# A fourth block by half-size products: the second half batch of the first expert, with its sums of x made earlier

## The chip, the cores and the metric

The kernel runs on one core of a Trainium2 chip. Its time is the device time in microseconds (us) of one execution, as the median of several runs. The engines are TensorE (PE in the rows; PEld is its weight load), VectorE (DVE), ScalarE (ACT), GpSimd (POOL) and SyncE (SP), which issues the DMAs. Each works through its own queue in order; semaphores tie them together.

## The reference

Three layers follow one another: banded attention, a mixture of eight experts with gates normalised eight times by rows and columns, and a gated linear unit. The change lies in the first expert.

```python
logits = x @ w_gate                      # x: 1536 tokens x 512
P = np.exp(logits - logits.max())
for _ in range(8):
    P /= P.sum(1, keepdims=True) + 1e-09
    P /= P.sum(0, keepdims=True) + 1e-09
    P *= N / E
for e in range(E):                       # 8 experts
    h = np.maximum(x @ w1[e], 0.0)       # w1[e]: 512 x 1024
    ye = h @ w2[e]                       # w2[e]: 1024 x 512
    out += P[:, e:e + 1] * ye
```

## The kernel before

**Numbers in two parts.** Every float32 operand is split into a high part, rounded by ScalarE's copy, and a low part, which GpSimd gets by a subtraction (`split_one`, L222). A product takes three matmuls: high by high, high weights by low tokens, low weights by high tokens (`product`, L376; L382, L383, L384). The low part of the weights is so first read by the third matmul of a product. `wh`, `wl` are the parts of weights, `xh`, `xl` those of x, `hh`, `hl` those of the hidden layer.

**Visits.** An expert's 1024 hidden units are four blocks `f` of 256. A visit is one block over a set of tokens: the first layer (x by `w1`), relu, and the second layer (by `w2`), which adds into `acc`, 128 tokens at a time (a unit). A unit is 6 matmuls of 512 columns. The units of a visit are done during the next one. The list `visits` (L161) sets the order. For the first expert, before:

- visits 0 to 3: blocks 0 to 3 over the first 384 tokens of batch 0 (beside the attention);
- visits 4 to 7: blocks 3 to 0 over its other 384 tokens;
- visit 8: block 0 over all 768 tokens of batch 1, in two chunks, with the weights of visit 7 still in place;
- visits 9 to 11 (`H0` to `F0`): blocks 1, 2, 3 over batch 1, by half-size products.

From visit 12 on every visit of the other experts does both batches by half-size products.

**Two ways for the first layer.** The plain way (`run_visit`) takes 24 matmuls of 384 columns per chunk of 384 tokens, 48 for 768 tokens. The other (`pair`, L517) cuts weights and tokens into two by two blocks and does seven products instead of eight (`run(0)` to `run(6)`, 6 matmuls each, 42 in all). It needs seven left factors, made of the weights: four sums and differences of blocks (`sum_steps`, L280, on GpSimd, into `sg`), and seven splits (`form_step`, L291: ScalarE writes `wh`, GpSimd `wl`). And it needs right factors, made once per half batch of x (`trans_steps`, L1435): four whole blocks (L1452) and four differences (L1457) on VectorE, and four splits, three into `th`, `tl` and one back into a block of `xh`, `xl`. `trans_steps(1)` is for batch 1, `trans_steps(0)` for batch 0.

**What sets the order.** The order of each engine's queue is the order in which the code issues. Side work is cut into steps; a tick after each piece of TensorE's work issues some. `Paced` spreads its steps evenly over a number of ticks; `Planned` has a count for each tick. Up to visit 8 there are three such lists: `ahead` (the weights of the next visit), `side` (the gate's normalisation) and `other` (the sums of x). From visit 9 on `run_half` has its own list `ahead` and the ticks of `side`. `load` (L199) issues the two DMAs of 512 KB for the next weights on the SP queue, in order, each waiting until the old weights of that buffer have been read.

Of the kernel before, what the change touches and what calls it, by code (L numbers as in the profile page):

```python
# [81 lines left out]
def tile_global_local_attention__then__sinkhorn_moe__then__glu(  # L82
# [37 lines left out]
    CB = S // C  # L120
    FQ = 2 * P
    NQ = F // FQ
# [31 lines left out]
    def acc(t):  # L154
        return accs[t // TB][:, t % TB, :]
# [3 lines left out]
    chunks = [(t, 4) for t in range(0, NT, 4)]  # L159
    halves = [[(b * TB + t, TC) for t in range(0, TB, TC)] for b in range(B)]  # L160
    visits = []  # L161


    up, down = list(range(NQ)), list(reversed(range(NQ)))
    for order, over in (
        (up, halves[0][:1]), (down, halves[0][1:]), (down[3:], halves[1])
    ):
        for n, f in enumerate(order):
            again = len(visits) >= NQ and n < 2
            visits.append(  # L170
                dict(
                    kind="moe", e=0, f=f, chunks=over, slot=(len(visits) + len(visits) // NQ) % 2,
                    load=not again, start=n == 0,
                )
            )
    H0 = len(visits)
    for f in (down[2], *up[2:]):
        visits.append(
            dict(kind="fast", e=0, f=f, slot=len(visits) % 2, load=True, kept=f == down[2])
        )  # L180
    F0 = len(visits)
    for e in range(1, E):
        for f in range(NQ):
            visits.append(dict(kind="fast", e=e, f=f, slot=len(visits) % 2, load=True))
    for f in range(NFF):
        slot = 1 - visits[-1]["slot"]
        visits.append(dict(kind="gate", f=f, piece=3 * f))
        visits.append(dict(kind="val", f=f, piece=3 * f + 1, slot=slot))
    NA = NQ + 1
    NB0 = CB * NQ  # L190
# [8 lines left out]
    def load(b):  # L199
        at = state["load", b]  # L200
        state["load", b] += 1
        if at == len(queues[b]):
            for i in range(2):
                load_piece(2 * b + i)
            return
        for j, src in enumerate(queues[b][at]):
            nc.sync.dma_start(
                out=raw[b][:, j * 4 * FQ : (j + 1) * 4 * FQ].rearrange(
                    "p (k f) -> p k f", k=src.shape[0] // P
                ),  # L210
                in_=src.rearrange("(k p) f -> p k f", p=P),
            )
# [9 lines left out]
    def split_one(r, h, lo, eng=nc.gpsimd):  # L222
        nc.scalar.activation(out=h, in_=r, func=AF.Copy)  # L223
        eng.tensor_tensor(out=lo, in0=r, in1=h.bitcast(F32), op=ALU.subtract)  # L224
# [10 lines left out]
    def second_steps(n):  # L235

        vis = visits[n]
        if vis["kind"] == "gate" or vis.get("kept"):
            return
        if vis["kind"] == "val":  # L240
            r = piece(vis["piece"] + 1)
        else:
            r = raw[vis["raw"]][:, 4 * FQ : 8 * FQ]
        eng = nc.vector if n == G0 + 1 else nc.gpsimd
        yield from split_halves(r, wh[vis["slot"]][1], wl[vis["slot"]][1], eng)

    def first_steps(n):

        vis = visits[n]
        if vis["load"]:  # L250
            r = raw[vis["raw"]][:, 0 : 4 * FQ]
            yield from split_halves(r, wh[vis["slot"]][0], wl[vis["slot"]][0])

    def ahead_steps(n):


        if 1 < n < H0 - 1:
            yield from first_steps(n + 1)
        if visits[n]["load"]:
            yield from second_steps(n)  # L260
            yield lambda b=visits[n]["raw"]: load(b)
        if n == 1:
            yield from first_steps(n + 1)

    def form(i):
        a, col = (1, i) if i < 4 else (0, i - 4)
        cols = slice(col * FQ, (col + 1) * FQ)
        return wh[a][0][:, cols], wl[a][0][:, cols]

    def w1_blocks(n):  # L270
        r = first_raw(n).rearrange("p (k f c) -> p f k c", k=KD, f=2)
        return {(i, j): r[:, i, 2 * j : 2 * j + 2, :] for i in range(2) for j in range(2)}

    def tall(ap):
        return ap.rearrange("p (k c) -> p k c", k=2)

    def sums():
        return [tall(state["sums"][:, i * FQ : (i + 1) * FQ]) for i in range(4)]

    def sum_steps(n):  # L280

        a, (s1, s2, s3, s4) = w1_blocks(n), sums()
        for out, x, y, op in (
            (s1, a[1, 0], a[1, 1], ALU.add), (s2, s1, a[0, 0], ALU.subtract),
            (s4, a[0, 1], s2, ALU.subtract), (s3, a[0, 0], a[1, 0], ALU.subtract),
        ):
            yield lambda out=out, x=x, y=y, op=op: nc.gpsimd.tensor_tensor(
                out=out, in0=x, in1=y, op=op
            )

    def form_step(n, i):  # L291
        a, (s1, s2, s3, s4) = w1_blocks(n), sums()
        src = (a[0, 0], s1, s2, s4, s3, a[0, 1], a[1, 1])[i]
        h, lo = form(i)
        split_one(src, tall(h), tall(lo))
# [144 lines left out]
    def unit_second(n, t, at, j):  # L440
        vis = visits[n]
        ps = state["Y"].next()
        second(vis, hid[at], j, ps)
        a = acc(t)
        if vis["kind"] != "val":
            if n == H0 - 1:
                nc.scalar.activation(out=a, in_=ps, func=AF.Copy)
            elif vis.get("start"):
                nc.vector.tensor_copy(out=a, in_=ps)
            elif vis["e"] == 0:  # L450
                nc.vector.tensor_tensor(out=a, in0=ps, in1=a, op=ALU.add)
            else:
                gate = state["gate"]
                e = vis["e"]
                if e == 1 and vis["f"] == 0:
                    nc.vector.tensor_scalar(
                        out=a, in0=a, scalar1=gate[:, t, 0:1], scalar2=None, op0=ALU.mult
                    )
                nc.vector.scalar_tensor_tensor(  # L459
                    out=a, in0=ps, scalar=gate[:, t, e : e + 1], in1=a,  # L460
                    op0=ALU.mult, op1=ALU.add,
                )
        elif vis["f"] == 0:
            nc.vector.tensor_copy(out=a, in_=ps)
        elif vis["f"] < NFF - 1:
            nc.vector.tensor_tensor(out=a, in0=ps, in1=a, op=ALU.add)
        else:
            nc.vector.tensor_tensor(out=a, in0=ps, in1=a, op=ALU.add)
            nc.sync.dma_start(out=out[t * P : (t + 1) * P, :], in_=a)
# [11 lines left out]
    def flush(tick):  # L481
        pending, state["pending"] = state["pending"], []
        for unit in pending:
            unit_second(*unit)
            tick()
# [198 lines left out]
    def run_half(n, side):  # L684

        ahead = list(sum_steps(n + 1))
        if not visits[n]["kept"]:
            ahead += [*second_steps(n), lambda: load(visits[n]["raw"])]

        def slots(i):  # L690
            side()
            if ahead:
                ahead.pop(0)()
            if i:
                form_step(n + 1, i - 1)

        pair(n, 1, slots, {1: 1, 2: 1, 3: 1, 4: 1, 5: 2})
        for step in ahead:
            step()
        form_step(n + 1, 6)  # L700
# [75 lines left out]
    with tc.tile_pool(name="attn", bufs=1) as ap:  # L776
# [473 lines left out]
        with tc.If(banded > 0) as cmp:  # L1250
            with tc.tile_pool(name="banded", bufs=1) as fp:
# [30 lines left out]
                side = steps[begin + 1 :]  # L1282
                side = Planned(side, [0, *[1] * len(side)])
# [7 lines left out]
        with cmp.Else():  # L1291
            with tc.tile_pool(name="whole", bufs=1) as gp:
# [15 lines left out]
                for s in range(B * NP):  # L1308
# [17 lines left out]
                    for i in range(NB):  # L1326
# [29 lines left out]
                        for j in range(2):  # L1356
# [13 lines left out]
                            e = ga["e"]  # L1370
# [29 lines left out]
        kept = ["pending", "hid", ("load", 0), ("load", 1)]  # L1400
# [16 lines left out]
    fast = ctx.enter_context(tc.tile_pool(name="fast", bufs=1))  # L1417
    work = fast.tile([P, 8 * C], F32, name="work")
    kept = fast.tile([P, 6 * C], F32, name="kept")
# [144 lines left out]
                yield divided  # L1564

    first_, second_ = trans_steps(1), trans_steps(0)
    side = Paced(gate_steps(), 5 * (NB0 - NA) + 5 * CB + 13 * (F0 - H0) - 4)
    other = Planned([*first_[:-1], *second_], [2, 1] * 3 + [1] * 14)

    def both():  # L1570
        side.tick()
# [2 lines left out]
    for n in range(NA, H0):  # L1574
        if n < H0 - 1:
            run_visit(n, both, ahead_steps(n))
        else:
            ahead = [*sum_steps(H0), *(lambda i=i: form_step(H0, i) for i in range(4))]
            run_visit(n, both, ahead, pace=12)
    other.finish()  # L1580
    for i in range(4, 7):
        form_step(H0, i)
    first_[-1]()
    load(visits[H0]["raw"])

    state["after"], state["lows"] = [[] for _ in range(7)], []
    state.update(X=Ring(bank[0:2]), P2=bank[2], P5=bank[3], Y=Ring(bank[4:7]), G=Ring([bank[7]]))
    for n in range(H0, F0):
        run_half(n, side.tick)
    side.finish()  # L1590

    state["sums"] = work[:, 8 * FQ : 12 * FQ]
    state["Y"] = Ring(bank[4:8])
# [62 lines left out]
```

## Time and profile before

| | |
|---|---|
| three runs, median | 1387.54 us (1387.25 to 1387.89) |
| the profiled execution, its own time | 1388.02 us |
| its span, first to last instruction | 1386.2 us |
| TensorE busy | 1379.5 us |
| VectorE, GpSimd, ScalarE busy | 921.5, 667.9, 575.2 us |

The span is what the hardware profiler saw between the first and the last instruction; the execution's own time is 1.8 us more. Matmuls are pipelined: a row's duration overlaps the next row's, and what a matmul takes of TensorE's time is the step from its start to the next one's.

### The profile page before, as it was taken

How to read it: one execution, taken by the hardware profiler on the slowest of the kernel's cores; microseconds unless marked ns; L12 is line 12 of the kernel's file. 1: busy time of each engine (PE TensorE's matmuls, PEld its weight loads, DVE VectorE, ACT ScalarE, POOL GpSimd, SP SyncE). 2: the span in 40 equal slices, each digit the busy share in tenths (PEclk: the TensorE clock that was granted, in tenths of full speed). 3: DMA queues.
4: the chain of work that ended last, by engine and by line, in shares of the span. 5: the costliest groups of instructions: out<-in, count | busy, mean ns of one | idle time of the engine just before them, and what ended most of it. 6: DMA issues, size and time to landing. Idle time of an engine off the chain costs nothing.

```text
span 1386.2 us, 20767 instructions
## 1 busy us (share of the span) xinstructions
PE 1379.5 (100%) x7407; PEld 1233.9 (89%) x7407; DVE 921.5 (66%) x1770; ACT 575.2 (41%) x1372; POOL 667.9 (48%) x787
## 2 busy tenths in 40 slices
PE   9999999999999999999999999999999999999999
PEld 5888899999999999999999999999999899999998
DVE  7775866867666676767676676667665674555446
ACT  7785453333333333333333333333333464434441
POOL 5763685454445434454454444545453374443440
PEclk9999999999999999999999999999999999999999
DMA  7860112121213212121213212122120001010002
GB/s 172 206 163 13 61 62 77 53 77 54 76 54 107 73 57 76 54 77 54 77 54 107 77 54 76 55 75 71 59 91 31 16 32 46 16 47 31 31 1 92
DMA packets 99889, 93.73 MB, mean 68 GB/s; under 512 B 55104, under 2 KB 74304, under 8 KB 99776
## 3 DMA queue, kind: packets, MB, share of 16 engines
q1 hardware_dynamic: 98688, 91.98, 21.6%
q8 instruction: 60, 0.98, 0.3%
q14 instruction: 53, 0.43, 0.1%
q10 hardware_dynamic: 1088, 0.33, 0.1%
HBM read 79.71 MB, written 12.58 MB: 67 GB/s over the span
## 4 chain that ended last, share of the span: by engine, by line
PE 99%; DMA 1%; SPq 0%; issue 0%; ACTq 0%; DVE 0%; ACT 0%
PE bank L382 31%; PE bank L384 31%; PE bank L383 31%; PE bank L1078 2%; PE bank L1143 2%; PE bank L1128 1%; PE bank L934 1%; PE bank L713 0%; DMA kr<-in_k_dram 0%; DMA vo<-in_v_dram 0%; PE bank L1486 0%; PE bank L1490 0%; PE bank L835 0%; PE bank L1538 0%; SPq L794 0%
## 5 line engine op out<-in xcount | busy, mean ns | idle before, releaser
L459 DVE SCALAR_TENSOR_TENSOR acc<-bank,gate,acc 128x512 f32<-128x512 f32 x336 | 251.5, 749 | 228.5 <-PE bank L384 222.7
L224 POOL TENSOR_TENSOR wl<-raw,wh 128x256 fp32r<-128x256 f32 (+1 forms) x222 | 222.0, 1016 | 314.9 <-ACT wh L223 299.9
L382 PE MATMUL bank<-wh,hh 128*128 128x512 f32 x914 | 358.8, 393 | 0.0
L384 PE MATMUL bank<-wh,hl 128*128 128x512 f32 x914 | 357.6, 391 | 0.0
L383 PE MATMUL bank<-wl,hh 128*128 128x512 f32 x914 | 356.3, 390 | 0.0
L382 PE MATMUL bank<-xh,wh 128*128 128x384 f32 x744 | 252.0, 339 | 0.3 <-issue 0.3
L383 PE MATMUL bank<-xl,wh 128*128 128x384 f32 x744 | 249.9, 336 | 0.0
L384 PE MATMUL bank<-xh,wl 128*128 128x384 f32 x744 | 249.4, 335 | 0.0
L583 ACT ACTIVATE hh<-kept 128x384 fp32r<-128x384 f32 x177 | 92.9, 525 | 325.4 <-DVE kept L593 325.4
L384 PEld LDWEIGHTS bank<-wh,hl 128*128 128x128 f32 x914 | 171.5, 188 | 37.8
L224 POOL TENSOR_TENSOR wl<-work,wh 128x256 fp32r<-128x256 f32 x156 | 126.4, 814 | 149.4 <-ACT wh L223 149.3
L597 ACT ACTIVATE kept<-bank 128x384 f32<-128x384 f32 x249 | 122.0, 491 | 174.2 <-PE bank L384 172.8
L382 PEld LDWEIGHTS bank<-wh,hh 128*128 128x128 f32 x914 | 171.7, 188 | 22.5 <-issue 0.2
L383 PEld LDWEIGHTS bank<-wl,hh 128*128 128x128 f32 x914 | 171.8, 188 | 22.5
L382 PE MATMUL bank<-th,wh 128*128 128x384 f32 x498 | 167.7, 337 | 0.0
L384 PE MATMUL bank<-th,wl 128*128 128x384 f32 x498 | 167.3, 336 | 0.0
L383 PE MATMUL bank<-tl,wh 128*128 128x384 f32 x498 | 167.0, 335 | 0.0
L593 DVE TENSOR_TENSOR kept<-bank,kept 128x384 f32<-128x384 f32 x249 | 137.3, 552 | 38.4 <-PE bank L384 36.9
L382 PEld LDWEIGHTS bank<-xh,wh 128*128 128x128 f32 x744 | 139.7, 188 | 9.9 <-issue 0.9
L383 PEld LDWEIGHTS bank<-xl,wh 128*128 128x128 f32 x744 | 139.8, 188 | 9.3
L384 PEld LDWEIGHTS bank<-xh,wl 128*128 128x128 f32 x744 | 139.8, 188 | 0.0
L585 DVE SCALAR_TENSOR_TENSOR hl<-kept,hh 128x384 fp32r<-128x384 f32 x177 | 120.6, 682 | 1.9 <-ACT hh L583 1.8
(168 smaller groups left out, 1724.9 us busy)
## 6 DMA issues: line engine op xcount, KB each, us to landing
raw<-in_moe_w_dram SPq DMA_DIRECT2D x74, 512.0 KB, 4.3
glw<-work SPq DMA_DIRECT2D x36, 256.0 KB, 2.3
raw<-glw SPq DMA_DIRECT2D x18, 512.0 KB, 3.5
work<-in_moe_w_gate_dram SPq DMA_DIRECT2D x12, 512.0 KB, 3.8
work<-in_moe_w_val_dram SPq DMA_DIRECT2D x12, 512.0 KB, 4.0
work<-in_moe_w_out_dram SPq DMA_DIRECT2D x12, 512.0 KB, 3.8
qr<-in_q_dram SPq DMA_DIRECT2D x32, 96.0 KB, 2.8
vo<-in_v_dram SPq DMA_DIRECT2D x32, 96.0 KB, 2.7
```

Source lines behind the costliest of these rows:

```text
L224: eng.tensor_tensor(out=lo, in0=r, in1=h.bitcast(F32), op=ALU.subtract)
L382: nc.tensor.matmul(lhsT=ah, rhs=bh, start=first, stop=False, **mm)
L383: nc.tensor.matmul(lhsT=ah, rhs=bl, start=False, stop=False, **mm)
L384: nc.tensor.matmul(lhsT=al, rhs=bh, start=False, stop=end, **mm)
L459: nc.vector.scalar_tensor_tensor(out=a, in0=ps, scalar=gate[:, t, e : e + 1], in1=a, op0=ALU.mult, op1=ALU.add,)
L583: nc.scalar.activation(out=hh, in_=src, func=AF.Relu)
L585: lambda: nc.vector.scalar_tensor_tensor(out=hl, in0=src, scalar=0.0, in1=hh.bitcast(F32), op0=ALU.max, op1=ALU.subtract,)
L593: nc.vector.tensor_tensor(out=p, in0=ps, in1=kept, op=ALU.add)
L597: nc.scalar.activation(out=snap[:, i], in_=ps, func=AF.Copy)
L934: nc.tensor.transpose(ps[:, j * P : (j + 1) * P], raw_[u % QKB][:, j, :], ident)
L1078: nc.tensor.matmul(out=ps[j][:, lo:KW], lhsT=qT[rows, own], rhs=kT[rows, i % UB, lo:KW], start=True, stop=True,)
L1143: nc.tensor.matmul(out=ps[j * D : (j + 1) * D, at * P : (at + 1) * P], lhsT=vo[p][:, a, i - 1 + a, j, :], rhs=aT[:, j, a, :], start=(a == ...
```

## The change

Visit 8 is done by half-size products too. The list of visits loses its third group, and `H0` becomes 8; the half-size visits over batch 1 are now blocks 1, 0, 2, 3 (visits 8 to 11). `trans_steps(1)` is issued whole in visits 5 to 7, with the first six steps of `trans_steps(0)` behind it; the last six of that are issued in visits 8 to 11, at every eighth tick. The sums and the first four left factors of visit 8 are issued in visit 7, behind visit 7's own weights. Blocks 1 and 0 keep their `w2`, and their `w1` is loaded again. ScalarE's copy of a first result (L447) moves from visit 8's to the new visit 8's units. The slots of the weights swap.

```diff
     for order, over in (
-        (up, halves[0][:1]), (down, halves[0][1:]), (down[3:], halves[1])
+        (up, halves[0][:1]), (down, halves[0][1:])
     ):
...
-                    kind="moe", e=0, f=f, chunks=over, slot=(len(visits) + len(visits) // NQ) % 2,
+                    kind="moe", e=0, f=f, chunks=over, slot=len(visits) % 2 ^ (len(visits) >= NQ),
...
-    for f in (down[2], *up[2:]):
+    for f in (*down[2:], *up[2:]):
         visits.append(
-            dict(kind="fast", e=0, f=f, slot=len(visits) % 2, load=True, kept=f == down[2])
+            dict(
+                kind="fast", e=0, f=f, slot=1 - len(visits) % 2, load=True,
+                start=f == down[2], kept=f in down[2:],
+            )
         )
...
-            visits.append(dict(kind="fast", e=e, f=f, slot=len(visits) % 2, load=True))
+            visits.append(dict(kind="fast", e=e, f=f, slot=1 - len(visits) % 2, load=True))
...
-            if n == H0 - 1:
+            if n == H0:
                 nc.scalar.activation(out=a, in_=ps, func=AF.Copy)
...
         ahead = list(sum_steps(n + 1))
-        if not visits[n]["kept"]:
+        if n > H0:
             ahead += [*second_steps(n), lambda: load(visits[n]["raw"])]
...
-    side = Paced(gate_steps(), 5 * (NB0 - NA) + 5 * CB + 13 * (F0 - H0) - 4)
-    other = Planned([*first_[:-1], *second_], [2, 1] * 3 + [1] * 14)
+    side = Paced(gate_steps(), 5 * (NB0 - NA) + 13 * (F0 - H0) - 4)
+    other = Planned([*first_, *second_[:6]], [2, 1] * 3 + [1] * 9)
...
-            ahead = [*sum_steps(H0), *(lambda i=i: form_step(H0, i) for i in range(4))]
+            ahead = [
+                *ahead_steps(n), *sum_steps(H0), *(lambda i=i: form_step(H0, i) for i in range(4)),
+            ]
             run_visit(n, both, ahead, pace=12)
     other.finish()
     for i in range(4, 7):
         form_step(H0, i)
-    first_[-1]()
     load(visits[H0]["raw"])
...
+    other = Planned(second_[6:], [0, 0, 0, 0, 1, 0, 0, 0] * 6)
     for n in range(H0, F0):
-        run_half(n, side.tick)
+        run_half(n, both)
     side.finish()
+    other.finish()
```

In the rows that follow a matmul line of the changed kernel is three higher than before (L384 is L387). GpSimd before, from visit 6's last weights (`wl_87`) over visit 7's (`wl_85`) to the first left factor of visit 9 (`wl_86` with 256 columns):

```order
L224 TENSOR_TENSOR wl_87<-raw_88,wh_83 128x512
L224 TENSOR_TENSOR wl_85<-raw_89,wh_81 128x512 x2
L224 TENSOR_TENSOR tl<-work,th 128x2x384
L287 TENSOR_TENSOR sg<-raw_88 128x256
L224 TENSOR_TENSOR tl<-work,th 128x2x384
L287 TENSOR_TENSOR sg<-sg,raw_88 128x256
L287 TENSOR_TENSOR sg<-raw_88,sg 128x256
L224 TENSOR_TENSOR tl<-work,th 128x2x384
L287 TENSOR_TENSOR sg<-raw_88 128x256
L224 TENSOR_TENSOR xl<-work,xh 128x2x384
L224 TENSOR_TENSOR wl_86<-raw_88,wh_82 128x256
```

GpSimd now, the same stretch, up to the first left factor of the new visit 8:

```order
L227 TENSOR_TENSOR wl_87<-raw_88,wh_83 128x512
L227 TENSOR_TENSOR xl<-sg,xh 128x2x384
L227 TENSOR_TENSOR wl_85<-raw_89,wh_81 128x512 x2
L290 TENSOR_TENSOR sg<-raw_88 128x256
L290 TENSOR_TENSOR sg<-sg,raw_88 128x256
L290 TENSOR_TENSOR sg<-raw_88,sg 128x256
L290 TENSOR_TENSOR sg<-raw_88 128x256
L227 TENSOR_TENSOR wl_86<-raw_88,wh_82 128x256
```

The split of batch 1's fourth factor (`xl<-sg`) stands ahead of visit 7's weights; batch 0's splits (`tl`, `xl<-work`) are gone from here. TensorE before, from visit 7's last unit into the old visit 8, whose weights (`wh_80`, `wl_84`) are those of visit 7:

```order
L384 MATMUL bank_68<-wh_83,hl_79 128x512
L1538 MATMUL bank_69<-gate,ones 128x117
L382 MATMUL bank_63<-xh,wh_80 128x384
L383 MATMUL bank_63<-xl,wh_80 128x384
L384 MATMUL bank_63<-xh,wl_84 128x384
```

TensorE now, from the same unit into the new visit 8:

```order
L386 MATMUL bank_68<-wl_87,hh_78 128x512
L387 MATMUL bank_68<-wh_83,hl_79 128x512
L385 MATMUL bank_63<-xh,wh_82 128x384
L386 MATMUL bank_63<-xl,wh_82 128x384
L387 MATMUL bank_63<-xh,wl_86 128x384
```

The third matmul of the new visit 8 reads `wl_86`, the last row of GpSimd's list; the gate's matmul has moved behind this product. VectorE before, from the first hidden half of visit 7 (`hl_79<-bank_64`) to its last unit's sum (the last row); `work<-xh,xl` are whole blocks, `work<-work` differences of `trans_steps(0)`:

```order
L433 SCALAR_TENSOR_TENSOR hl_79<-bank_64,hh_78 128x384
L1528 TENSOR_REDUCE rsum<-gate 128x12
L1531 RECIPROCAL rsum<-rsum 128x12
L1532 TENSOR_TENSOR gate<-gate,rsum 128x12x8
L1452 TENSOR_TENSOR work<-xh,xl 128x768
L433 SCALAR_TENSOR_TENSOR hl_79<-bank_65,hh_78 128x384
L1452 TENSOR_TENSOR work<-xh,xl 128x768
L451 TENSOR_TENSOR acc_77<-bank_66,acc_77 128x512
L1457 TENSOR_TENSOR work<-work 128x768
L451 TENSOR_TENSOR acc_77<-bank_67,acc_77 128x512
L1457 TENSOR_TENSOR work<-work 128x768
L451 TENSOR_TENSOR acc_77<-bank_68,acc_77 128x512
```

VectorE now, from behind the same first half:

```order
L1455 TENSOR_TENSOR work<-xh,xl 128x768
L436 SCALAR_TENSOR_TENSOR hl_79<-bank_65,hh_78 128x384
L1531 TENSOR_REDUCE rsum<-gate 128x12
L1534 RECIPROCAL rsum<-rsum 128x12
L1535 TENSOR_TENSOR gate<-gate,rsum 128x12x8
L1455 TENSOR_TENSOR work<-xh,xl 128x768
L454 TENSOR_TENSOR acc_77<-bank_66,acc_77 128x512
L1455 TENSOR_TENSOR work<-xh,xl 128x768
L454 TENSOR_TENSOR acc_77<-bank_67,acc_77 128x512
L1460 TENSOR_TENSOR work<-work 128x768
L454 TENSOR_TENSOR acc_77<-bank_68,acc_77 128x512
L1460 TENSOR_TENSOR work<-work 128x768
```

Each whole block and difference of batch 0 stands one piece of visit 7 later than before.

## Rows read from the trace of the kernel before

**Rows 1.** The page: busy time of the engines; the chain that ended last, by engine
```profile
PE 1379.5 (100%) x7407; PEld 1233.9 (89%) x7407; DVE 921.5 (66%) x1770; ACT 575.2 (41%) x1372; POOL 667.9 (48%) x787
...
PE 99%; DMA 1%; SPq 0%; issue 0%; ACTq 0%; DVE 0%; ACT 0%
```
**Rows 2.** TensorE's waits: line, releaser: us in total, times, longest
```profile
PE bank L951 <- DMA kr<-in_k_dram: 1.4, 1, 1.4
...
PE bank L382 <- issue: 0.3, 1, 0.3
```
**Rows 3.** TensorE's timeline, visit 7 into visit 8: start, us, engine, line, operation
```profile
157.31 0.33 PE L382 MATMUL bank<-xh,wh 128*128 128x384 f32 x1
...
160.77 0.34 PE L384 MATMUL bank<-xh,wl 128*128 128x384 f32 x1
160.94 0.39 PE L382 MATMUL bank<-wh,hh 128*128 128x512 f32 x1
...
164.81 0.39 PE L384 MATMUL bank<-wh,hl 128*128 128x512 f32 x1
165.04 0.37 PE L1538 MATMUL bank<-gate,ones 128*128 128x117 f32 x2
```
**Rows 4.** One stretch: length, busy PE, PEld, DVE, ACT, POOL, clock, DMA, GB/s
```profile
148.48:163.73 15.25, 15.25 (x86) 13.34 (x85) 11.67 (x18) 8.30 (x15) 15.16 (x9) 1.00 0.07 20
```
**Rows 5.** GpSimd's timeline, 148 to 181 us
```profile
148.48 1.83 POOL L224 TENSOR_TENSOR tl<-work,th 128x768 fp32r<-128x768 f32 x1 [4.74 <-ACT th L223]
...
155.43 1.28 POOL L224 TENSOR_TENSOR wl<-raw,wh 128x512 fp32r<-128x512 f32 x1
...
156.67 2.57 POOL L224 TENSOR_TENSOR tl<-work,th 128x768 fp32r<-128x768 f32 x1
...
159.21 2.01 POOL L224 TENSOR_TENSOR wl<-raw,wh 128x512 fp32r<-128x512 f32 x1
...
174.56 1.39 POOL L287 TENSOR_TENSOR sg<-raw,sg 128x256 f32<-128x256 f32 x1
...
178.41 1.85 POOL L224 TENSOR_TENSOR xl<-work,xh 128x768 fp32r<-128x768 f32 x1
...
180.94 0.74 POOL L224 TENSOR_TENSOR wl<-sg,wh 128x256 fp32r<-128x256 f32 x1
```
**Rows 6.** One line's instructions: durations in ns, min/median/max, first and last start
```profile
L287 POOL TENSOR_TENSOR sg<-raw,sg x4: 737/742/1386, 174.6 to 214.5; 128x256 f32<-128x256 f32 x4
```
**Rows 7.** VectorE's timeline, 155 to 169 us
```profile
155.70 1.82 DVE L1452 TENSOR_TENSOR work<-xh,xl 128x768 f32<-128x768 f32 x1
...
158.12 1.95 DVE L1452 TENSOR_TENSOR work<-xh,xl 128x768 f32<-128x768 f32 x1
...
162.50 2.04 DVE L1452 TENSOR_TENSOR work<-xh,xl 128x768 f32<-128x768 f32 x1
...
166.40 0.94 DVE L1457 TENSOR_TENSOR work<-work 128x768 f32<-128x768 f32 x1
...
167.87 0.94 DVE L1457 TENSOR_TENSOR work<-work 128x768 f32<-128x768 f32 x1
```
**Rows 8.** DMA issues from 143.5 to 150 us: count, size, median us to landing
```profile
raw<-in_moe_w_dram SPq DMA_DIRECT2D x1, 512.0 KB, 3.4
```
**Rows 9.** TensorE's timeline at the kernel's start (windows of growing length)
```profile
1.19 0.61 PE L835 MATMUL bank<-zeros 128*128 128x512 bf16 x1 [1.19 <-DVE zeros L831]
...
1.19 3.16 PE L835 MATMUL bank<-zeros 128*128 128x512 bf16 x7 [1.19 <-DVE zeros L831]
...
1.19 3.59 PE L835 MATMUL bank<-zeros 128*128 128x512 bf16 x9 [1.19 <-DVE zeros L831]
...
6.85 0.30 PE L951 MATMUL bank<-ident,kr 128*128 128x128 f32 x1 [1.43 <-DMA kr<-in_k_dram]
...
8.25 0.61 PE L835 MATMUL bank<-zeros 128*128 128x512 bf16 x2
```
**Rows 10.** The start as one stretch, columns as in rows 4
```profile
1.19:4.40 3.21, 3.21 (x9) 1.17 (x10) 0.71 (x2) 1.49 (x2) 1.54 (x13) 1.00 0.25 48
```
**Rows 11.** Groups by line and shape, 150 to 200 us: busy, mean ns
```profile
L447 ACT ACTIVATE acc<-bank 128x512 f32<-128x512 f32 x6 | 3.6, 594 | 1.7 <-PE bank L384 1.7
```

## The prediction

> **What bounds the kernel now.** I read the engine table and the chain first: TensorE is busy 1379.5 of 1386.2 us and holds 99% of the chain that ended last [rows 1]. Then who TensorE waited for: its longest wait is 1.4 us on a DMA at the very start; around the change there is only 0.3 us of "issue" [rows 2]. So every matmul taken out shortens the span, and every wait that is put in front of TensorE lengthens it one for one. The next view is TensorE's timeline where the change sits: visit 7, the last over the first half batch, ends at 165.04 us, and visit 8 starts there without a gap [rows 3]. The last views are those of GpSimd and VectorE in the same stretch: GpSimd is busy 15.16 of 15.25 us between 148.48 and 163.73 us [rows 4], so it finishes what it owes visit 7 only 1.3 us before visit 8 starts. What is added to its queue in that stretch comes out late by its whole length.
>
> **What is removed.** Visit 8's first layer was 48 matmuls of 384 columns and is now 42 (seven products, two halves, three passes). Their price is not the 0.34 us that a row shows, since neighbours overlap, but the step from one start to the next: from 157.31 to 160.77 us are 20 steps, 0.173 us each [rows 3]. Six of them: **-1.04 us**. The second layer, 36 matmuls of 512 columns, stays; a step of it is 0.228 us (160.94 to 164.81, 17 steps) [rows 3].
>
> **What is added in front of TensorE.** The old visit 8 reused weights already in place, so nothing had to be made for it. The new one needs seven left factors (four sums of weight blocks, three plain blocks), each split into a high and a low part, and TensorE's third matmul of the visit reads the low part of the first factor, which GpSimd writes. GpSimd's queue after visit 6's last weights is now: the low part of the fourth factor of x (moved here from behind visit 8), visit 7's two second weights, four sums of blocks, then that first low part. All of them are in order, on one engine.
>
> Undelayed durations: 1.85 us for a low part of 768 elements, 1.28 for 512, 0.74 for 256 [rows 5], 0.742 median for a sum [rows 6]. So 1.85 + 2 x 1.28 + 4 x 0.74 + 0.74 = 8.1 us.
>
> The start: visit 6's last weights end at 159.21 + 2.01 = 161.2 us in the trace [rows 5]. VectorE's first whole block of x (the row at 155.70) moves from before them to beside the next, which spares the 2.57 us operation at 156.67 its delay; by the undelayed 1.83 at 148.48 that is 0.74 us [rows 5]. So about 160.45, and the first low part is done at 168.6 us at the earliest.
>
> VectorE is in the way, too. Where one of its operations with two SBUF inputs of 768 elements stands beside GpSimd, both come out longer: VectorE's 1.82, 1.95 and 2.04 us instead of 0.94 [rows 7], GpSimd's 2.57 instead of 1.83, 2.01 instead of 1.28, 1.39 instead of 0.74 [rows 5]. They end one behind the other, as if each waited for the other's instruction to end; each such meeting costs GpSimd 0.65 to 0.74 us. After 160.45 the new order has five of these on VectorE (three whole blocks, two differences), each a tick later than before, one behind each piece of visit 7. In the trace the two differences at 166.40 and 167.87 ran in 0.94, GpSimd being idle then [rows 7]; now it is not. Five times 0.7 is 3.5 us, so the low part is there at 172.1 us.
>
> TensorE can do two matmuls from 165.04 and stands at the third from 165.4 us: a wait of **6.7 us**. The ends: 3.2 us with no meeting at all (168.6), 7.5 with six meetings, the gate's small product being the sixth. I take 6.7, since the rows show a delay at nearly every meeting. Nothing else is late there: ScalarE is busy 8.30 of 15.25 us [rows 4], and the weights that the sums read are loaded long before (the one 512 KB issue between 143.5 and 150 us, landed after 3.4 us) [rows 8].
>
> **The pace after the wait.** TensorE has no such gap in this trace. At the very start it had done nothing: its first seven 512-column matmuls start 0.425 us apart ((3.16 - 0.61) / 6), the next two 0.215 apart, though the clock column reads 1.00 for that stretch [rows 9, 10]; 512 columns in those times are the 1.2 and the 2.4 GHz level. After a gap of 1.43 us the two at 8.25 take 0.61 together, full pace [rows 9]. A gap of 6.7 us lies far beyond the second case, and I take the first: 7 x 0.21 = **+1.5 us**, with ends of zero and twice that (an estimate). The Trainium skill ("TensorE: Matmul & The Clock Gate", section "HAM oscillation — how this bites in real kernels") says that a wait for data that leaves TensorE idle long enough drops its clock to half, and that the matmuls behind it pay for it; by that rule the sum is the one above, without it 1393.2. No wait of that length stands in this trace, so it neither bears the rule out nor refutes it.
>
> **What costs nothing, and its cover.** The first results of the second half batch are copied by ScalarE, six in visit 9 where there were three in 8 and three in 9; at 0.594 us each [rows 11] that is 3.6 us in a visit of 42 x 0.173 + 36 x 0.228 = 15.5 us. The four low parts of the other half's factors (1.85 each) now lie in visits 8 to 11. The fullest is visit 11: eleven operations of 0.74, two of 1.28 and two of 1.85 are 14.4 us of GpSimd against 15.5 of TensorE. If delays push it over, the next visit's sums are made a visit ahead of their use, so one or two us late still costs nothing. The tightest place is visit 9's third product: GpSimd gets to its weights at 172.1 + 6 x 0.74 + 7 x 0.74 + 1.85 = 183.6 us, TensorE at about 172.1 + (40 x 0.173 + 18 x 0.228) + 2 x 1.04 + 1.37 = 186.6. That leaves 3 us. One more load of weights on the SP queue (1 MB) goes out two visits ahead of its use.
>
> **The sum.** The profiled execution took 1388.02 us: -1.04 + 6.7 + 1.5 gives 1395.2. The median of the three runs is 0.48 us lower, so I predict **1394.7 us**, slower by 0.5%.
>
> **Rivals.**
> - *The wait without the slow pace behind it.* For it: full pace after 1.43 us. Against: the start of the kernel. 1387.54 - 1.04 + 6.7 = 1393.2.
> - *A short wait.* VectorE's operations fall between GpSimd's or behind its sums; TensorE waits 3.2 to 4 us at full pace. For it: after visit 7's last unit VectorE has little left, so late ones may slip behind. Against: in the trace almost every meeting delays. 1387.54 - 1.04 + 3.2 = 1389.7, up to 1390.5.
> - *No wait, the other side.* If GpSimd had its low part ready by 165.4 us, the six matmuls would be all that is left: 1386.5, no change that can be told. It decides at 3.2 us: GpSimd would have to start its run that much earlier than 148.48. Its first operation there waits for ScalarE, which waits for VectorE's first difference, and none of these moves. Against it is the sum, in which nothing is left to take away.
> - *A second wait.* GpSimd stays behind: with three more delays of 0.74 in visit 8 and the low part of 1.85 in its way, visit 9's third product is late, and so on through visit 11. Each miss costs 1 to 2 us: 1397 to 1399.
>
> **How the numbers follow.** The forecast 0.49, without the slow pace 0.27, the short wait 0.12, no wait 0.04, a second wait 0.08. A measurement of this kernel can tell 0.2% (2.8 us) from no change: slower begins at 1390.3, faster at 1384.7. Same holds "no wait" mostly and two thirds of the short wait: 0.12. Faster needs gains that no row shows: 0.02. Slower: 0.86. The range leaves out "no wait", some of the second wait and the longest slow pace: 1389.6 to 1397.0.
>
> **What would show it.** Right: in TensorE's waits one new line, the third matmul of the first half-size product on GpSimd's low part (the line of the product's last pass), 6 to 7.5 us once, near 165 us; GpSimd without a gap from 148.5 to beyond 172; no further wait from there to the end, and every later visit as long as before. The step between matmuls behind the wait says which level the clock had: 0.32 for 384 columns or 0.173. Wrong: no wait line over 1 us there, or a first low part that is done before 168 us; or waits in visits 9 to 12.

## The result, and the profile after

| | before | after |
|---|---|---|
| median, us | 1387.61 (6 runs, 1387.25 to 1388.08) | 1396.21 (6 runs, 1395.49 to 1396.95) |
| profiled execution, us | 1388.02 | 1396.06 |
| its span, us | 1386.2 | 1394.2 |

The changed kernel is slower: ratio 1.0062, 95% interval [1.0049, 1.0075]. The forecast was 1394.7 in a range of 1389.6 to 1397.0.

The page of the changed kernel has six matmuls fewer than before, as the diff says, and GpSimd in the chain, where it was not [rows 1]:

```profile
PE 1382.1 (99%) x7401; PEld 1235.2 (89%) x7401; DVE 923.0 (66%) x1773; ACT 579.3 (42%) x1382; POOL 678.2 (49%) x798
...
PE 98%; POOL 1%; DMA 0%; issue 0%; ACT 0%; DVE 0%; ACTq 0%; DVEq 0%
```

TensorE's waits (line, releaser: us in total, times, longest) have one new line, and none of the other lines is longer than 1.2 us:

```profile
PE bank L387 <- POOL wl L227: 6.4, 1, 6.4
PE bank L838 <- DVE zeros L834: 1.2, 1, 1.2
```

TensorE's timeline there, to be held against [rows 3]: the third matmul of the new visit 8 waits, and the steps behind it are long:

```profile
164.68 0.34 PE L386 MATMUL bank<-xl,wh 128*128 128x384 f32 x1
171.45 0.69 PE L387 MATMUL bank<-xh,wl 128*128 128x384 f32 x1 [6.43 <-POOL wl L227]
171.94 0.52 PE L385 MATMUL bank<-xh,wh 128*128 128x384 f32 x1
172.26 0.52 PE L386 MATMUL bank<-xl,wh 128*128 128x384 f32 x1
...
176.10 0.63 PE L387 MATMUL bank<-wh,hl 128*128 128x512 f32 x1
176.52 0.46 PE L385 MATMUL bank<-wh,hh 128*128 128x512 f32 x1
176.82 0.40 PE L386 MATMUL bank<-wl,hh 128*128 128x512 f32 x1
177.05 0.39 PE L387 MATMUL bank<-wh,hl 128*128 128x512 f32 x1
```

Without the wait the third matmul would have started one step behind the second, at 164.85; it started at 171.45, so the wait is 6.6 us. From there a 384-column step is 0.32 us (171.94 to 172.26) and a 512-column step 0.43 (176.10 to 176.52), nearly twice the 0.173 and 0.228 of [rows 3]; from 176.8 on the 512-column steps are 0.23 again. The stretches (length, busy PE, PEld, DVE, ACT, POOL, clock, DMA, GB/s, as in rows 4) show GpSimd without a gap, TensorE idle, and then the clock at half (the trace has it at 0.50 from 169.8 us, while TensorE still stands, to 176.6; hence the 0.88 of the second line):

```profile
148.48:163.73 15.25, 15.25 (x85) 13.52 (x85) 11.31 (x19) 9.36 (x17) 15.21 (x10) 1.00 0.16 54
166.00:171.00 5.00, 0.00 (x0) 0.00 (x0) 3.45 (x5) 1.50 (x4) 4.84 (x5) 0.88 0.31 105
171.00:173.00 2.00, 1.55 (x5) 1.55 (x6) 0.00 (x0) 0.78 (x3) 2.00 (x4) 0.50 0.00 0
...
177.00:179.00 2.00, 2.00 (x11) 1.80 (x11) 1.45 (x4) 0.48 (x2) 2.00 (x4) 1.00 0.99 357
```

GpSimd's timeline answers to rows 5. From 159.91 on stands the chain that the prediction added up, and the low part that TensorE waits for ends at 171.40:

```profile
159.91 2.58 POOL L227 TENSOR_TENSOR xl<-sg,xh 128x768 fp32r<-128x768 f32 x1
162.45 3.26 POOL L227 TENSOR_TENSOR wl<-raw,wh 128x512 fp32r<-128x512 f32 x2
165.67 1.43 POOL L290 TENSOR_TENSOR sg<-raw 128x256 f32<-128x256 f32 x1
167.18 1.39 POOL L290 TENSOR_TENSOR sg<-sg,raw 128x256 f32<-128x256 f32 x1
168.65 1.39 POOL L290 TENSOR_TENSOR sg<-raw,sg 128x256 f32<-128x256 f32 x1
170.00 0.72 POOL L290 TENSOR_TENSOR sg<-raw 128x256 f32<-128x256 f32 x1
170.68 0.72 POOL L227 TENSOR_TENSOR wl<-raw,wh 128x256 fp32r<-128x256 f32 x1
```

Five of these are long: 2.58 for 1.85, 1.99 for 1.28 (one of the two in the 3.26), 1.43, 1.39 and 1.39 for 0.74. Beside them stand VectorE's five sums of x, three whole blocks and two differences; the whole blocks are lengthened too [rows 7]:

```profile
159.53 1.25 DVE L1455 TENSOR_TENSOR work<-xh,xl 128x768 f32<-128x768 f32 x1
...
162.53 2.05 DVE L1455 TENSOR_TENSOR work<-xh,xl 128x768 f32<-128x768 f32 x1
...
165.09 1.42 DVE L1455 TENSOR_TENSOR work<-xh,xl 128x768 f32<-128x768 f32 x1
...
167.04 0.94 DVE L1460 TENSOR_TENSOR work<-work 128x768 f32<-128x768 f32 x1
...
168.51 0.94 DVE L1460 TENSOR_TENSOR work<-work 128x768 f32<-128x768 f32 x1
```

**Where the time went.** The six matmuls -1.04, the wait +6.6, the slow pace +2.4 (from the third matmul to the sixth of 512 columns 177.05 - 171.45 = 5.60 us; at full pace the same took 3.20, in the second run with filling below): +7.96. Counting TensorE's matmuls one by one, the changed kernel ends visit 7 0.5 us earlier (164.50 against 165.04 in [rows 3], which no part of the change explains; the trace before has two short stalls that the other lacks, at 33.1 us on a DMA and at 132.8 us, the "issue" of [rows 2]), needs 8.2 us more from there to the kernel's last matmul, and 0.3 more behind that; the two profiled executions differ by 8.04. Of the 8.2, 0.2 is not in the sum; 0.1 of it is the first step behind a wait, which takes 0.28 us for 0.17 in that run with filling too. Nothing is added later: VectorE's instructions on two landmarks (lines 459 and 481, before 456 and 478) start at 250.2 and 1390.1 us instead of 242.6 and 1382.4, 7.6 and 7.7 later.

### The profile page after: what moved, and what is told of

Same layout as the page of the kernel before. It is cut to its first block, busy times and chain, and to the rows that moved or that the text cites. A ratio compares the mean times of both kernels' runs of the same rounds, so it can differ in the third digit from the quotient of the medians.

```text
span 1394.2 us, 20799 instructions
## 1 busy us (share of the span) xinstructions
PE 1382.1 (99%) x7401; PEld 1235.2 (89%) x7401; DVE 923.0 (66%) x1773; ACT 579.3 (42%) x1382; POOL 678.2 (49%) x798
## 4 chain that ended last, share of the span: by engine, by line
PE 98%; POOL 1%; DMA 0%; issue 0%; ACT 0%; DVE 0%; ACTq 0%; DVEq 0%
PE bank L385 30%; PE bank L387 30%; PE bank L386 30%; PE bank L1081 2%; PE bank L1146 2%; PE bank L1131 1%; PE bank L937 1%; POOL wl L227 0%; PE bank L716 0%; DMA kr<-in_k_dram 0%; POOL sg L290 0%; PE bank L1489 0%; PE bank L1493 0%; POOL xl L227 0%; PE bank L838 0%
## 5 line engine op out<-in xcount | busy, mean ns | idle before, releaser
L227 POOL TENSOR_TENSOR wl<-raw,wh 128x256 fp32r<-128x256 f32 (+1 forms) x225 | 225.4, 1018 | 318.6 <-ACT wh L226 303.7
L387 PE MATMUL bank<-wh,hl 128*128 128x512 f32 x914 | 357.9, 392 | 0.0
L387 PE MATMUL bank<-xh,wl 128*128 128x384 f32 x736 | 247.4, 336 | 6.4 <-POOL wl L227 6.4
L387 PEld LDWEIGHTS bank<-wh,hl 128*128 128x128 f32 x914 | 171.6, 188 | 37.9
L387 PE MATMUL bank<-th,wl 128*128 128x384 f32 x504 | 169.7, 337 | 0.0
L387 PEld LDWEIGHTS bank<-xh,wl 128*128 128x128 f32 x736 | 138.4, 188 | 7.0 <-POOL wl L227 6.8
```

What stands on the lines that cost most here:

```text
L387: nc.tensor.matmul(lhsT=al, rhs=bh, start=False, stop=end, **mm)
```

## The experiments

My theory: TensorE waits for GpSimd's chain, which is in order and lengthened by the meetings with VectorE; then it pays for having stood still with half its clock. Each time below is a median; the kernel before had 1387.49 (21 runs, 1387.22 to 1389.14) beside the sums later, the split alone, the factors first and the first filling, and 1387.83 (21 runs, 1387.11 to 1390.26) beside the other four.

**The other half's sums later.**

```diff
-    other = Planned([*first_, *second_[:6]], [2, 1] * 3 + [1] * 9)
+    other = Planned(first_, [2, 1] * 3 + [1] * 3)
...
-    other = Planned(second_[6:], [0, 0, 0, 0, 1, 0, 0, 0] * 6)
+    other = Planned(second_, [0, 0, 0, 1] * 12)
```

> All twelve steps of the other half's sums of x are issued in visits 8 to 11, so VectorE's three whole blocks and two differences no longer stand beside GpSimd's chain ahead of visit 8. Theory (GpSimd's chain in order, each of the five meetings with VectorE adding 0.7 us): the first low part is done near 171.4 - 5 x 0.7 - 0.5 = 167 to 168 us, TensorE waits 2 to 3 us at the third matmul of visit 8: 1387.6 - 1.04 + 2.4 = 1389.0 at full pace, 1391 if the clock falls all the same. Rival (the wait comes from the split of the fourth factor alone, the meetings cost nothing on the path): wait still 6.4 us, 1396. Rival (half-size visits over this half batch are dearer by themselves): the wait falls but the time stays above 1392.

Measured 1391.12 (1389.37 to 1391.67), ratio 1.0022 [1.0012, 1.0031]. TensorE's timeline in this run, with the wait in brackets:

```profile
167.20 0.44 PE L387 MATMUL bank<-xh,wl 128*128 128x384 f32 x1 [2.36 <-POOL wl L227]
167.48 0.33 PE L385 MATMUL bank<-xh,wh 128*128 128x384 f32 x1
167.65 0.33 PE L386 MATMUL bank<-xl,wh 128*128 128x384 f32 x1
```

and GpSimd's, where the operations of the chain have their undelayed length again:

```profile
159.03 1.85 POOL L227 TENSOR_TENSOR xl<-sg,xh 128x768 fp32r<-128x768 f32 x1
160.83 2.62 POOL L227 TENSOR_TENSOR wl<-raw,wh 128x512 fp32r<-128x512 f32 x2
163.41 0.74 POOL L290 TENSOR_TENSOR sg<-raw 128x256 f32<-128x256 f32 x1
```

The meetings were worth 6.43 - 2.36 = 4.1 us of the wait: the five, 3.4 us, and one just ahead of 159.91 (2.01 us for 1.28). Neither rival fits. Behind a wait of 2.4 us the steps stay at 0.17 us in this trace. The profiled execution took 1389.37, near the 1389.0 that the theory gave for full pace; but seven of the ten runs lay at 1390.7 to 1391.7, near the 1391 that it gave for a fallen clock, and no trace shows one of them. Two further traces were taken for that:

> The same kernel as the run with the sums later, for a second trace: its ten runs lay in two groups, three at 1389.4 to 1389.6 us (the profiled one, full pace behind a wait of 2.4 us) and seven at 1390.7 to 1391.7. If this run is of the upper group: theory (a wait of 2.4 us also costs the pace in some runs, for a shorter stretch): steps of 0.32 us behind 167.2 us, 1.5 to 1.8 us lost there. Rival (a late wait of VectorE's low parts near 1130 us, as in the run with the split alone moved): steps of 0.173 us behind the wait, and a wait line of 1.2 us on kept.

> As the run before it: a further trace of the same kernel, to have one of the upper group, with the same two readings.

Both fell in the lower group, 1389.66 and 1389.53 us, with waits of 2.4 and 2.3 us and full pace behind them. What the upper group loses is not shown. One thing on record points at the clock: the mean granted clock of the whole run is 0.999 in five of the seven, which is 0.7 to 2.1 us of full clock, and 1.000 in the three lower runs and in both further ones. So a wait of 2.4 us may bring the half pace in some executions and not in others; this is not shown, since two of the seven have 1.000, and one run with the factors first, without a wait and no longer than the others, has 0.999 as well.

**Only the split moved.**

```diff
-    other = Planned([*first_, *second_[:6]], [2, 1] * 3 + [1] * 9)
+    other = Planned([*first_[:-1], *second_[:6]], [2, 1] * 3 + [1] * 8)
...
         form_step(H0, i)
+    first_[-1]()
```

> Only the split of batch 1's fourth factor moves back behind the left factors; the other half's sums of x stay where the change put them. Theory: GpSimd's chain is shorter by 1.85 us, the five meetings stay, so TensorE waits 6.4 - 1.85 = 4.6 us: 1387.6 - 1.04 + 4.6 = 1391.2 at full pace, up to 1393.7 with the slow stretch of the changed kernel. Rival (this split is what sets the wait): no wait line over 1 us, 1386.6. Rival (the half-size visit is dearer by itself): over 1394.

Measured 1395.59 (1394.33 to 1396.86), ratio 1.0057 [1.0042, 1.0072]. The wait is what the theory said, and the half pace follows it:

```profile
169.39 0.69 PE L387 MATMUL bank<-xh,wl 128*128 128x384 f32 x1 [4.66 <-POOL wl L227]
169.88 0.53 PE L385 MATMUL bank<-xh,wh 128*128 128x384 f32 x1
170.20 0.53 PE L386 MATMUL bank<-xl,wh 128*128 128x384 f32 x1
```

The median is 1.9 us above the theory's upper number, 1393.7, and by the time alone the last reading (the half-size visit dearer by itself, over 1394) would fit; the trace decides against it. In this trace 1.45 us are lost elsewhere, at 1137 us: TensorE waits 1.22 us for VectorE, which is late from two low parts that it makes there itself. VectorE in this run, and then in the changed kernel:

```profile
1132.00 3.57 DVE L227 TENSOR_TENSOR wl<-raw,wh 128x512 fp32r<-128x512 f32 x2 [2.87 <-ACT wh L226]
```

```profile
1133.84 2.17 DVE L227 TENSOR_TENSOR wl<-raw,wh 128x512 fp32r<-128x512 f32 x2 [2.86 <-ACT wh L226]
```

Without it the run would be at 1394.1, which is the theory's 1391.2 with 2.6 us for the pace and the 0.25 that the changed kernel also has beyond its sum. A wait like it also stands in the first run with filling below (1.23 us at 1144 us) and in no other trace here, so it is not tied to this edit; whether the other three runs of this version have it is not shown. The rival that the split sets the wait falls: 4.7 us are left of 6.4.

**The factors first.** Besides what the first run moved, the split stands behind the factors, and in visit 7:

```diff
-                *ahead_steps(n), *sum_steps(H0), *(lambda i=i: form_step(H0, i) for i in range(4)),
+                *sum_steps(H0), *(lambda i=i: form_step(H0, i) for i in range(2)),
+                *ahead_steps(n), *(lambda i=i: form_step(H0, i) for i in range(2, 4)),
```

> The other half's sums of x wait for visits 8 to 11, the fourth factor's split stands behind the left factors, and in visit 7 the sums and the first two left factors of visit 8 are issued ahead of visit 7's second weights. Theory (the whole loss is the wait and the slow pace behind it): no wait over 1 us at visit 8, the six matmuls are the whole difference, 1387.6 - 1.04 = 1386.5. Rival (the half-size visit is dearer by itself): not under 1387.6, and more like 1389 to 1392. Rival (the chain only shifts: visit 7's second weights or visit 9's products become late): a new wait of 1 to 3 us there, 1388 to 1390.

Measured 1387.83 (1387.36 to 1389.47), ratio 1.0005 [0.9995, 1.0014]: the whole loss is gone, but no gain is left. The time alone would also fit the rival that the half-size visit is dearer by itself (not under 1387.6); the steps decide. From visit 8's start to the kernel's last matmul TensorE takes 0.06 us less than before. What its steps from 162 to 240 us take beyond full pace (0.173 and 0.228 us a step) adds up to 0.94 us more than before. -1.04 + 0.94 is -0.10, so the six matmuls are saved and 0.94 us is given back, 0.31 and 0.55 of it in two stalls, at 175.5 and 180.4. The second, on TensorE:

```profile
180.36 0.50 PE L387 MATMUL bank<-wh,hl 128*128 128x512 f32 x1 [0.28 <-DVE hl L588]
```

VectorE's queue ahead of it, where a sum of x that meets GpSimd's 1.88 us split takes 2.60 us and nothing over 0.04 us is idle from there to the stall:

```profile
169.91 2.60 DVE L1455 TENSOR_TENSOR work<-xh,xl 128x768 f32<-128x768 f32 x1
...
179.21 2.10 DVE L588 SCALAR_TENSOR_TENSOR hl<-kept,hh 128x384 fp32r<-128x384 f32 x2
```

The half-size visit is not dearer by itself. The meetings have only moved: what stood ahead of visit 8 now stands in it.

**The split behind the factors**, and the sums later as in the first run, the factors at the place of the change.

> The other half's sums of x wait for visits 8 to 11 and the fourth factor's split stands behind the left factors, with the factors' place behind visit 7's weights as in the change. Theory: the first low part is ready at 167.2 - 1.85 = 165.4 us, TensorE waits 0.5 to 0.6 us and keeps its pace: 1387.5 - 1.04 + 0.5 = 1387.0, with the 0.9 us that the run with the factors first lost in visit 8 up to 1387.9. Rival (a wait of any length brings the slow stretch): 1389.5 or more.

Measured 1388.95 (1388.52 to 1389.63), ratio 1.0006 [0.9996, 1.0015]. The wait is 0.92 us and the pace full:

```profile
166.02 0.45 PE L387 MATMUL bank<-xh,wl 128*128 128x384 f32 x1 [0.92 <-POOL wl L227]
```

The time is 1 us above the upper number that was named. In the trace TensorE takes 0.8 us more than before from visit 8's start on: -1.04, the wait and its first step (1.1), and stalls of 0.7. Against the 0.5 to 0.6 that was expected the wait is 0.4 longer, on GpSimd, whose chain, now shorter, waits for ScalarE for the first time:

```profile
159.70 2.55 POOL L227 TENSOR_TENSOR wl<-raw,wh 128x512 fp32r<-128x512 f32 x2 [0.37 <-ACT wh L226]
```

The rest of the 1 us is not explained: the median is 1.1 above the kernel before, the trace shows 0.8. The rival (the slow stretch after any wait) falls for a wait this short: the pace is full, and the mean granted clock is 1.000 in all ten runs.

**The sums spread wider.** The edit is shown against the run with the factors first.

```diff
-    other = Planned(second_, [0, 0, 0, 1] * 12)
+    other = Planned(second_, [0] * 13 + [0, 0, 1] * 12)
```

> As the run with the factors first, but the other half's sums of x start in visit 9, every third tick, and none in visit 8, where that run had two stalls of TensorE (0.31 and 0.55 us) behind VectorE's whole blocks. Theory (those stalls ate the six matmuls' 1.04 us): no stall in visit 8, the trace from visit 8's start to its end 1.04 us shorter than before, 1387.5 - 1.0 = 1386.5. Rival (any place beside half-size visits costs as much, since VectorE and GpSimd delay one another there too): the stalls come back in visits 9 to 11, 1387.3 to 1387.8. Rival (half-size visits over this half batch are dearer by themselves): visit 8 stays as long as before.

Measured 1387.77 (1386.99 to 1388.82), ratio 0.9998 [0.9989, 1.0007]. TensorE's stalls are smaller (0.22 us near 180, 0.18 near 228; by the same sum 0.50 us more than before, so -0.54 is left), and from visit 8's start to its last matmul it takes 0.49 us less than before; the median shows nothing of it. The expected 1386.5 was missed, and 1387.77 lies where the rival had it: about half of the stalls are gone, and the one near 180 stands where VectorE now has no sum of x. Of the versions tried this has the lowest median, and it is no faster than the kernel before.

**The gap filled, first try.** 26 matmuls of 512 columns are put ahead of visit 8's first product; nothing reads their result.

```diff
+        if n == H0:
+            for _ in range(26):
+                nc.tensor.matmul(
+                    out=bank[7], lhsT=wh[0][0][:, 0:P], rhs=xh[:, 0, 0:CM], start=True, stop=True
+                )
         run(0, x, block(0, 0))
```

> The changed kernel with 26 matmuls of 512 columns added ahead of visit 8's first product, whose result nothing reads; they fill some 5.9 of the 6.4 to 6.6 us that TensorE waits. Theory (the slow stretch of 5 us behind the wait comes from TensorE having been idle in it): the granted clock stays at 1.00 behind 171.4 us, the steps of 384 columns are 0.173 us, and the time falls by the 2.5 us that the slow stretch costs: 1396.2 - 2.5 = 1393.7. Rival (the slow steps come from something else, such as operands that arrive late or GpSimd and VectorE beside it): steps stay 0.32 us, 1396.2. Rival (the added matmuls delay the chain): more than 1396.5.

Measured 1402.20 (1401.72 to 1402.90), ratio 1.0104 [1.0089, 1.0120]. It filled nothing: the buffer that I took for the weights is that of visit 8's own fifth left factor, which ScalarE writes only behind the four sums, and the first added matmul waited for that:

```profile
171.30 7.55 PE L604 MATMUL bank<-xh,wh 128*128 128x512 f32 x26 [6.54 <-ACT wh L226]
178.69 0.34 PE L385 MATMUL bank<-xh,wh 128*128 128x384 f32 x1
178.86 0.33 PE L386 MATMUL bank<-xl,wh 128*128 128x384 f32 x1
```

It still tells something: the 26 took 178.69 - 171.30 = 7.39 us, and the visit's own matmuls behind them ran at full pace (0.17). So the slow stretch falls on whatever comes first behind the gap.

**The gap filled, second try**, with the high parts of x on both sides (`lhsT=xh[:, 0, 0:P]`).

> The filling again, with 26 added matmuls of 512 columns whose operands (high parts of x alone) have long been there, so that they start when visit 7 ends and fill 5.9 of the 6.4 us wait; nothing reads their result. Theory (the slow stretch comes from TensorE's idle time): the third matmul of visit 8 still starts at 171.4 us, but behind it the steps of 384 columns are 0.173 us, and the time falls by the 2.6 us that the slow stretch cost: 1396.2 - 2.6 = 1393.6. Rival (the slow steps belong to the half-size visit's own operands, or to what GpSimd and VectorE do beside it): steps of 0.32 us there, 1396.2.

Measured 1394.52 (1394.11 to 1394.73), ratio 1.0045 [1.0029, 1.0060]:

```profile
164.13 6.10 PE L604 MATMUL bank<-xh 128*128 128x512 f32 x26
...
171.15 0.44 PE L387 MATMUL bank<-xh,wl 128*128 128x384 f32 x1 [0.57 <-POOL wl L227]
171.43 0.34 PE L385 MATMUL bank<-xh,wh 128*128 128x384 f32 x1
171.60 0.34 PE L386 MATMUL bank<-xl,wh 128*128 128x384 f32 x1
...
174.35 0.39 PE L387 MATMUL bank<-wh,hl 128*128 128x512 f32 x1
```

The third matmul comes when it came before (171.15 for 171.45), and the steps behind it are 0.17 us, with the same operands and the same neighbours: the slow stretch was the price of standing still. From the third matmul to the sixth of 512 columns it is 174.35 - 171.15 = 3.20 us, against 5.60. The time falls by 1.7, not 2.6 as expected (the 2.6 was too high by 0.2 as well): a stall of 0.7 us, in visit 8 on VectorE's sums, is new in this trace.

**The chain longer.**

```diff
+        def last_put():
+            h, lo = block(0, 1)
+            split_one(r21, h, lo)
+            if b == 1:
+                nc.gpsimd.tensor_tensor(out=lo, in0=r21, in1=h.bitcast(F32), op=ALU.subtract)
...
-put(r21, *block(0, 1)),
+lambda: last_put(),
```

> The changed kernel with the low part of batch 1's fourth factor written twice by GpSimd, 1.85 us more in its chain ahead of visit 8 (2.6 if it meets one of VectorE's sums). Theory (in-order chain on GpSimd, nothing to spare): the wait grows one for one, 6.4 to 8.3 us, and the slow stretch stays what it was: 1396.2 + 1.85 = 1398.1. Rival (the wait is set through VectorE or ScalarE): wait 6.4 to 7, under 1397.

Measured 1398.60 (1398.03 to 1398.73), ratio 1.0072 [1.0057, 1.0088]. The wait, 2.0 us longer for 1.85 more work:

```profile
PE bank L387 <- POOL wl L227: 8.5, 1, 8.5
```

Near to one for one, as the theory has it, and the time is 0.5 us above the 1398.1 that was expected. The rival (the wait set through VectorE or ScalarE) falls.

## Why the prediction was right, and where its size was off

**The six matmuls, -1.04.** Right: in the two runs without a wait ahead of visit 8 (the factors first, the sums spread wider) it accounts for TensorE's time in the trace to 0.05 us, once the stalls are taken off.

**The wait, +6.7.** Right: 6.6, and by its parts. The chain starts at 159.91 instead of the 160.45 worked out (visit 7 ends 0.54 us earlier in this execution, at 164.50). The work in it is the 8.1 us of the sum, the five meetings cost 3.4 instead of 3.5, and the low part is done at 171.40 instead of 172.1. Moving one item at a time bears out the parts: without the meetings the wait is 2.4, without the split 4.7, with another split 8.5. The Trainium skill ("SBUF — State Buffer", section "Summary: rules for kernel authors") says that when VectorE reads two operands from SBUF while GpSimd reads it, the second to start is blocked until the first is finished; the trace agrees, with GpSimd's sums at 0.74 us alone and 1.39 to 1.43 beside VectorE's, each of them ending 0.6 us behind the end of VectorE's operation.

**The pace, +1.5.** This is the mis-sized term: 2.4 us measured. The prediction took over the number of slow steps from the kernel's start (seven of 512 columns). Here ten matmuls of 384 columns, two small ones, three of 512 and part of a fourth ran at half pace. Its upper end, 3, held. The number of slow steps was no constant even at the kernel's start: in the changed kernel's trace all eleven steps there are slow, 5.11 us for twelve matmuls where [rows 9] has nine in 3.59:

```profile
1.19 5.11 PE L838 MATMUL bank<-zeros 128*128 128x512 bf16 x12 [1.19 <-DVE zeros L834]
```

The clock column that read 1.00 there [rows 10] says nothing: the trace's first record of the clock is at 4.2 us before, where the steps become full, and at 6.0 us now, behind the start of the twelfth. That the gap causes the slow pace was an assumption then, and is shown now by the filled gap. The Trainium skill's rule that was weighed ("TensorE: Matmul & The Clock Gate", the section named in the prediction) agrees: the granted clock was 0.50 behind 6.4 us of idleness, and 1.00 when the gap was filled.

**What costs nothing.** Right for the changed kernel: no wait from visit 9 on, the third product of visit 9 included. But the cover is thin, as the runs that moved more of the sums into visits 8 to 11 show, with up to 0.9 us of stalls there. One reading was off: the 0.3 us of "issue" that stood as around the change [rows 2] lie at 132.8 us, 32 us ahead of it; nothing in the sum hangs on it.

**The sum.** The terms with their measured sizes give +7.96, the prediction had +7.2. The median came out 1.5 us above the forecast: 0.9 of it the pace, the rest within the spread of the runs (1395.49 to 1396.95). The two slowest of the six, 1396.56 and 1396.95, have a mean granted clock of 0.996, the other four 0.998, so part of that spread goes with the pace.

**The rivals.** The wait without slow pace (1393.2) is excluded by the half clock. The short wait and no wait are excluded by the trace; a second wait did not come in the changed kernel. The later waits in the experiments' traces are of another kind, on VectorE: 1.2 us near 1140 us in two of them, and 0.5 us or less in visit 8 in three.

## What to carry to other kernels

When work is given to an engine that has no gap ahead of a due time, add up its queue from the last idle moment, with what each neighbour on the shared path adds; here that gave the wait to 0.1 us. A gap in TensorE's work can have two prices, the wait and the pace behind it. And six matmuls fewer are worth a microsecond only if the seven operands that they need have a place to be made: no order tried here showed a gain in the median.

## What was not expected of the hardware

- The price of the half clock behind a gap differed: from the third matmul to the sixth of 512 columns the loss was 2.6 us after a wait of 4.7, 2.4 after 6.4 and 2.7 after 8.5 (5.83, 5.60 and 5.93 us instead of 3.20). In the first run with filling the 26 matmuls lost 1.5 us behind a wait of 6.5 (7.39 us instead of 5.93, 164.13 to the next start at 170.06). A longer gap was not dearer. The granted clock of these traces shows why: in all four it fell to 0.50 while TensorE still stood, and it was back at 1.00 some 5.7, 5.2, 6.0 and 2.9 us after the matmuls had started again. The price goes with that remainder, near to half of it.
- Behind waits of 0.6, 0.9 and 2.4 us the pace was full in every trace taken (one, one and three); for 2.4 us the longer runs without a trace leave it open whether it always is.
